# Spectral filter stage: planes loaded by halves, their negation on VectorE, a contiguous D eviction and a new order

## The chip, the core and the metric

The kernel runs on one core of a Trainium2 chip. The metric is the device time of one execution in microseconds. Three compute engines share the stage that the change touches: TensorE (PE), VectorE (DVE) and ScalarE (ACT). GpSimd (POOL) does small work and issues transfers on its own queue; SyncE (SP) issues the other transfers.

## The reference

Two blocks follow each other on a 2048 x 576 tensor. The change is in the first one, a global spectral filter.

```python
X = rfft2(layernorm(x).astype(float32), axes=(-2, -1))
W = w_r + 1j * w_i                       # 2048 x 289 each, bf16
h = x + irfft2(X * W, s=(S, D)).astype(bfloat16)
h2 = h + (gelu(n @ w_gate) * (n @ w_up)) @ w_down      # n = layernorm(h)
```

## The kernel before

Both transforms are matrix products. The spectrum is handled in 16 groups. For each group `i` the filter stage does the following: `D` (matmuls of the transform along d, evicted from PSUM to `CUS`), `B` (a 16-point transform, evicted to `YS`), `T` (the product with the filter, `TP`), `Z` (sums, `ZS` and `ZR`) and `V` (matmuls of the inverse 16-point transform, evicted to `V`). `R` does as `V` for the remaining columns of four groups at once, evicted to `VR`. `WS` holds three planes for each group: minus the imaginary part, the real part, the imaginary part. One product per group then gives the four terms of the complex multiplication.

```python
# SyncE's queue: the imaginary plane whole, then the real one; 18 loads each
for f in w_loads(1, 0, SP) + w_loads(1, 1, SP) + w_loads(0, 0, SP) + w_loads(0, 1, SP):
    f()
...
# D: the two banks (odd, even) one after the other, written with a step of two elements
ev(eng, CUS[:, s3, :, :].rearrange("p a (j r) -> p r a j", r=2), banks(b0, 2, 2 * HK)..., ...)
...
# GpSimd negates, group by group, then clears VR
for i in range(NG):
    P.op(POOL, ... tensor_scalar(WS[:, g, 0, :], WS[:, g, 2, :], -1.0, 1.0, op0=ALU.mult, op1=ALU.mult) ...)
    if i == NVZ:
        P.op(POOL, lambda g: g.memset(VR[:, :, :, :, :], 0.0), w=["Vz"])
for w in SEQF:            # the order of all operations of the stage
    ...
# next in GpSimd's queue: the first gate weights of the feed-forward block, 1.3 MB
for j in range(3):
    wg_load(j, j)
```

Operations are put into one queue for each engine in program order; each waits for the operations whose data it needs. So whatever stands later in an engine's program waits for what stands earlier, whether it needs it or not.

## Time and profile before

| | before |
|---|---|
| time, median | 496.69 us |
| first D matmul | 19.98 us |
| first product TP | 27.26 us |
| first matmul of the inverse transform (L684) | 52.44 us |
| first matmul of the feed-forward block (L824) | 64.77 us |
| from there to the end of the span | 430.13 us |

What precedes the first D matmul varies from one execution to another, 19.4 to 20.5 us. So I compare traces by one length: from the first D matmul to the first feed-forward matmul, 44.79 us here. I call it the stage length. It is a difference of two start times in the order of time of TensorE.

The busy time in two windows, up to L684 and from there to the feed-forward block, for the kernel before (columns: window, its length, then busy time and number of instructions of each engine, TensorE's granted clock, share of the DMA engines, GB/s):

```profile
20.00:52.40 32.40, 29.66 (x237) 21.71 (x234) 25.06 (x65) 29.19 (x52) 11.96 (x19) 1.00 0.58 171
52.40:64.80 12.40, 11.85 (x102) 8.68 (x104) 9.99 (x34) 10.25 (x24) 7.95 (x11) 1.00 1.02 363
```

In the first window VectorE is busy for 25.06 of 32.40 us, because it waits 6.70 us at the start. TensorE and ScalarE are busy for 29 us or more.

### The profile page before, as it was taken

To read this page: it belongs to the slowest core of one execution; us is meant where nothing else is said; L and a number is where in the kernel's file an instruction comes from. 1 tells how busy PE (TensorE), PEld (TensorE's weight loads), DVE (VectorE), ACT (ScalarE), POOL (GpSimd) and SP (SyncE) were. 2 spreads that over 40 slices of the span, in tenths; PEclk is the share of its full clock that TensorE was granted. 3 is DMA by queue.
4 is the path that set the end of the run, shared out by engine and by line. 5 is a ranking of instruction groups with operands and counts; after the bars stand their busy time and mean duration, and the time that the engine had idled before them with its cause. 6 is when DMAs were issued, how large, how long until landed. Compare 5 with 4: busy or idle time off the path is not lost.

```text
span 494.9 us, 9880 instructions
## 1 busy us (share of the span) xinstructions
PE 486.1 (98%) x4338; PEld 288.1 (58%) x4338; DVE 192.4 (39%) x418; ACT 158.9 (32%) x300; POOL 34.6 (7%) x53
## 2 busy tenths in 40 slices
PE   7999999999999999999999999999999999999998
PEld 3767655555588854444477744444677544444775
DVE  6679743444365644433311144333211233333111
ACT  6989865232312243232300033232100132233000
POOL 5750701000000010000000000000000000000000
DMA  8666898411000062000000001000000000000000
GB/s 276 163 188 215 277 350 275 178 25 27 4 13 13 19 191 60 19 9 1 1 13 19 18 15 23 19 1 1 7 19 12 14 1 1 1 1 2 12 19 19
DMA packets 27164, 31.26 MB, mean 63 GB/s; under 512 B 11664, under 2 KB 20112, under 8 KB 27120
## 3 DMA queue, kind: packets, MB, share of 16 engines
q1 hardware_dynamic: 24224, 18.68, 13.0%
q0 software_dynamic: 2896, 11.95, 7.1%
q8 instruction: 34, 0.56, 0.5%
q14 instruction: 10, 0.08, 0.1%
HBM read 26.28 MB, written 2.36 MB: 58 GB/s over the span
## 4 chain that ended last, share of the span: by engine, by line
PE 88%; DVE 4%; issue 1%; ACT 0%; DVEq 0%
PE PS L824 57%; PE PS L874 29%; DVE TP L594 1%; DVE VR L565 1%; PE PS L841 1%; PE PS L684 1%; PE PS L723 1%; DVE ZS L600 1%; DVE XO L726 0%; PE PS L855 0%; DVE ZR L603 0%; PE PS L610 0%; DVE HN L757 0%; PE PS L777 0%; DVE TM L734 0%
## 5 line engine op out<-in xcount | busy, mean ns | idle before, releaser
L824 PE MATMUL PS<-HT,WG 64*128 64x512 bf16 x2106 | 228.5, 376 | 0.0
L824 PEld LDWEIGHTS PS<-HT,WG 64*128 64x128 bf16 x2106 | 107.3, 94 | 119.8 <-issue 1.0
L833 ACT ACTIVATE GL<-PS 128x512 bf16<-128x512 f32 x144 | 85.9, 597 | 257.3 <-PE PS L824 243.4
L834 DVE TENSOR_TENSOR AT<-GL,PS 128x512 bf16<-128x512 bf16 x144 | 98.9, 687 | 175.0 <-ACT GL L833 175.0
L874 PE MATMUL PS<-WD,AT 128*128 128x288 bf16 (+2 forms) x1152 | 144.3, 286 | 0.0
L874 PEld LDWEIGHTS PS<-WD,AT 128*128 128x128 bf16 x1152 | 110.8, 98 | 30.7 <-ACT GL L833 1.3
L877 DVE TENSOR_TENSOR OS<-PS,XO 128x288 bf16<-128x288 f32 (+2 forms) x32 | 14.6, 457 | 100.3 <-PE PS L874 100.3
L824 PE MATMUL PS<-HT,WGX 64*128 64x512 bf16 x486 | 53.4, 376 | 0.0
L824 PEld LDWEIGHTS PS<-HT,WGX 64*128 64x128 bf16 x486 | 23.7, 94 | 28.8
L714 ACT ACTIVATE JD<-XO 128x576 bf16<-128x576 bf16 x8 | 5.5, 683 | 28.5 <-DVE XO L858 28.5
L594 DVE TENSOR_TENSOR TP<-YS,WS 128x1152 bf16<-128x1152 bf16 (+2 forms) x17 | 11.8, 715 | 6.8 <-DMA WS<-in_A_w_r_dram 6.7
L574 PE MATMUL PS<-FT,U 128*128 128x288 bf16 x96 | 14.1, 286 | 0.1
L565 ACT ACTIVATE CUS<-PS 128x576 bf16<-128x576 f32 x16 | 13.5, 862 | 0.5 <-PE PS L574 0.4
L565 ACT ACTIVATE YS<-PS 128x576 bf16<-128x576 f32 x16 | 11.3, 705 | 2.3 <-DVE TP L594 2.2
L520 PE MATMUL PS<-ATS,XO 128*128 128x128 bf16 (+1 forms) x128 | 10.1, 221 | 1.7 <-POOL XN L534 1.1
L584 PE MATMUL PS<-CUS,BT 128*128 128x288 bf16 x64 | 10.5, 286 | 1.2 <-ACT YS L565 0.9
L464 DVE BATCH_NORM_STATS2 ST<-XO 128x6 f32<-128x288 bf16 x24 | 9.3, 438 | 4.5 <-DMA XO<-in_A_x_dram 4.5
L574 PEld LDWEIGHTS PS<-FT,U 128*128 128x128 bf16 x96 | 9.1, 98 | 2.9 <-ACT CUS L565 0.4
L520 PEld LDWEIGHTS PS<-ATS,XO 128*128 128x128 bf16 (+1 forms) x128 | 7.4, 97 | 4.7 <-POOL XN L534 1.6
L610 PE MATMUL PS<-VT,ZS 128*128 128x256 bf16 x64 | 9.0, 273 | 1.1 <-DVE VR L565 0.5
L565 ACT ACTIVATE V<-PS 128x512 bf16<-128x512 f32 (+1 forms) x17 | 10.0, 639 | 0.3 <-PE PS L610 0.2
L757 DVE TENSOR_SCALAR HN<-XO,TM,RS 128x576 bf16<-128x576 bf16 (+1 forms) x32 | 10.0, 361 | 0.0
(77 smaller groups left out, 215.0 us busy)
## 6 DMA issues: line engine op xcount, KB each, us to landing
WD<-in_B_w_down_dram POOLq DMA_DIRECT2D x9, 576.0 KB, 21.4
WG<-in_B_w_gate_dram POOLq DMA_DIRECT2D x4, 1152.0 KB, 9.7
WG<-in_B_w_up_dram SPq DMA_DIRECT2D x4, 1152.0 KB, 7.9
out_dram<-OS SPq DMA_DIRECT2D x30, 72.0 KB, 1.6
XO<-in_A_x_dram SPq DMA_DIRECT2D x3, 576.0 KB, 7.4
WGX<-in_B_w_gate_dram POOLq DMA_DIRECT2D x1, 1152.0 KB, 6.9
WGX<-in_B_w_up_dram SPq DMA_DIRECT2D x1, 1152.0 KB, 10.8
HT<-HN SPq DMA_TRANSPOSE x60, 2.4
```

What stands on the lines that cost most here:

```text
L464: P.op(DVE, lambda v, c=c, h=h: v.bn_stats(ST1[:, c, h, :], XO[:, c, 288 * h:288 * h + 288]), r=[("X", c)], w=[("ST1", c, h)])
L520: P.op(PE, lambda t, b=b, lhs=lhs, p0=p0, p1=p1, s=s, e=e, o=o, c=c: t.matmul(bank(b, p0, p1, o, o + 128), lhs, ATS[:, c, :], start=s, sto ...
L565: fn = (lambda v: v.tensor_copy(dst, src)) if eng == DVE else (lambda a: a.activation(dst, src, ACTF.Copy))
L574: P.op(PE, lambda t, b=b, m=m, us=us, o=o, g=g: t.matmul(bank(b, 0, 128, 0, 2 * HK), U[:, us, g, :, :], FT[:, 3 * o + (2 if us == 4 else u ...
L584: P.op(PE, lambda t, b=b, tb=tb, m=m, s3=s3, sp_=sp_: t.matmul(bank(b, 0, 128, 0, KW), BT[:, sp_, tb, :], CUS[:, s3, m, :], start=(m == 0) ...
L594: P.op(DVE, lambda v: v.tensor_tensor(TP[:, sl, :, :, q0:q1], y4, w4, op=ALU.mult), r=[("Y", sl), ("Wn", i)] + wkeys[0 if 1 <= g < 9 else ...
L757: P.op(eng, lambda v, c=c, hs=hs, o0=o0, o1=o1, x0=x0, x1=x1: v.tensor_scalar(HN[:, hs, o0:o1], XO[:, c, x0:x1], TM[:, 1, c:c + 1], RS2[:, ...
L824: op = P.op(PE, lambda t, h0=h0, kt=kt, wt=wt, b=b, s=(not second and j == 0), e=(second and j == n - 1): t.matmul(bank(b), wg_tile(slot)[ ...
L833: P.op(ACT, lambda a: a.activation(GL[:, s2, :], bank(b0), ACTF.Gelu_apprx_tanh), r=[("PS", b0)], w=[("GL", s2)])
L834: P.op(DVE, lambda v: v.tensor_tensor(AT[:, f, :], GL[:, s2, :], bank(b0 + 1), op=ALU.mult), r=[("GL", s2), ("PS", b0 + 1)], w=[("AT", f)])
L874: P.op(PE, lambda t, b=b, d0=d0, d1=d1, f=f, p=p: t.matmul(bank(b, 0, 128, 0, d1 - d0), AT[:, f, 128 * p:128 * p + 128], WD[:, f, d0:d1], ...
L877: P.op(DVE, lambda v, b=b, d0=d0, d1=d1, p=p, c=c: v.tensor_tensor(OS[:, p % 2, d0:d1], bank(b, 0, 128, 0, d1 - d0), XO[:, c, d0:d1], op=A ...
```

## The change

Its intent: load the first half of both planes before the second half, so that the first product need not wait for ten loads that it does not use (the second half of the imaginary plane); take the negation off GpSimd and do it in a few large operations on VectorE; write the D eviction contiguously; spread evictions over both engines and find the orders again.

```diff
-    for f in w_loads(1, 0, SP) + w_loads(1, 1, SP) + w_loads(0, 0, SP) + w_loads(0, 1, SP):
+    for f in w_loads(1, 0, SP) + w_loads(0, 0, SP):
+        f()
+    P.dma(SP, VT..., "vt", w=["VT"])          # moved here from ahead of the planes
+    for f in w_loads(1, 1, SP) + w_loads(0, 1, SP):
         f()
...
-        ev(eng, CUS[...].rearrange("p a (j r) -> p r a j", r=2), banks(...).rearrange("p r (a j) -> p r a j", a=2),
+        ev(eng, CUS[...].rearrange("p a (j r) -> p a j r", r=2), banks(...).rearrange("p r (a j) -> p a j r", a=2),
...
+    def st_w(i):
+        for g0, g1 in (((1, 5),), ((5, 9),), ((9, 13),), ((13, 16), (0, 1)))[i]:
+            P.op(DVE, ... tensor_scalar(WS[:, g0:g1, 0, :], WS[:, g0:g1, 2, :], -1.0, None, op0=ALU.mult),
+                 r=[k for k in wkeys[i // 2] if k[2] == 1], w=[("Wn", 4 * i + k) for k in range(4)])
...
-    for i in range(NG):
-        P.op(POOL, ... 16 negations ...)
-        if i == NVZ:
-            P.op(POOL, lambda g: g.memset(VR[:, :, :, :, :], 0.0), w=["Vz"])
+    P.op(POOL, lambda g: g.memset(VR[:, :, :, :, :], 0.0), r=[("ATS", c) for c in range(NT)], w=["Vz"])
...
-SEQF = """D0 D1 B0 D2 D3 T0 B1 D4 ... Z15b Z15a R3 V15 R4"""
+SEQF = """w0 D0 D1 D2 B0 B1 w1 T0 T1 D3 D4 Z0 B2 B3 Z1 D5 T2 T3 B4 w2 Z2 T4 ... V14 V15 R4 R3"""
+# and a table of the engine of each eviction: VectorE takes one D, two B, three V and seven VR
```

(The last V eviction is now one operation.)

## The prediction

> **What bounds the kernel now.** First the page, its chain that ended last, to see who sets the end.
>
> ```profile
> PE 88%; DVE 4%; issue 1%; ACT 0%; DVEq 0%
> PE PS L824 57%; PE PS L874 29%; DVE TP L594 1%; DVE VR L565 1%; PE PS L841 1%; PE PS L684 1%; PE PS L723 1%; DVE ZS L600 1%; DVE XO L726 0%; PE PS L855 0%; DVE ZR L603 0%; PE PS L610 0%; DVE HN L757 0%; PE PS L777 0%; DVE TM L734 0%
> ```
>
> 85% of the span is the feed-forward part (L824, L874), TensorE back to back, which the change does not touch. The same chain in order of time shows where it can act:
>
> ```profile
> 51.91 0.39 ACT V L565
> 52.30 0.14 issue
> 52.44 1.63 PE PS L684 x12
> ...
> 64.77 70.11 PE PS L824 x648
> ```
>
> The filter ends at 52.44 us, when the inverse transform (L684) may start; 12.3 us later TensorE starts the feed-forward part and no longer waits. So the change is worth what it moves that 52.44, microsecond for microsecond, if the 12.3 us after it stay. Before 51.9 the chain is almost all VectorE: TP (spectrum times filter), ZS and ZR (sums), VR (a cast). Next VectorE in order of time:
>
> ```profile
> 18.16 2.40 DVE L529 CAST U<-PS 128x384 bf16<-128x384 f32 x5
> 27.26 1.43 DVE L594 TENSOR_TENSOR TP<-YS,WS 128x1152 bf16<-128x1152 bf16 x2 [6.70 <-DMA WS<-in_A_w_r_dram]
> ```
>
> VectorE finishes the first transform at 20.56 and stands idle 6.70 us until the first half of the real filter plane lands. Then it works almost without a gap until 52.95. Meanwhile ScalarE goes from 21.07 to 52.57 with 2.9 us idle. The groups by shape in the first 130 us give the pieces:
>
> ```profile
> L565 ACT ACTIVATE CUS<-PS 128x576 bf16<-128x576 f32 x16 | 13.5, 862 | 0.5 <-PE PS L574 0.4
> L565 ACT ACTIVATE YS<-PS 128x576 bf16<-128x576 f32 x16 | 11.3, 705 | 2.3 <-DVE TP L594 2.2
> L594 DVE TENSOR_TENSOR TP<-YS,WS 128x1152 bf16<-128x1152 bf16 x15 | 10.9, 751 | 6.8 <-DMA WS<-in_A_w_r_dram 6.7
> L565 DVE CAST VR<-PS 32x256 bf16<-32x256 f32 x15 | 6.3, 418 | 0.3
> L632 POOL TENSOR_SCALAR WS<-WS 128x288 bf16<-128x288 bf16 x16 | 6.9, 431 | 2.2 <-DVE ATS L494 0.9 <-POOL WS L632 0.2
> ```
>
> These durations overlap by some 0.1 us; for a queue I take start to start from the order of time: CUS 0.67, YS 0.52, V 0.47, TP 0.68, ZS plus ZR 0.44, VR 0.43 us, and on TensorE 0.73 (D), 0.49 (B), 0.45 (V) and 0.22 (R).
>
> **What the Trainium skill says.** "VectorE: DVE Perf Modes", The perf-mode tier table: a one-source bf16 operation within SBUF may run four elements a cycle, and one reading PSUM may not. The trace agrees: in the same window, HN at L757 averages 424 ns for 576 columns and 303 for 64, so 0.24 ns a column. "SBUF — State Buffer", Who interferes with whom: such an operation shares a port pair with GpSimd, and the second to issue blocks until the first ends; the trace of before has no such pair on which I could test it. "PSUM — Partial Sum Buffer", Specifications: cachelines are 8 bytes and non-contiguous patterns slow matmuls. It says nothing of evictions that hop between two banks; no run here shows it yet. "DMA: Bandwidth & Descriptors", Queues, rings and completion order: engines take turns between queue rows by packet, yet a completion increment waits for earlier writes of the engine across its queues. The trace shows the delay, whichever of the two makes it:
>
> ```profile
> WS<-in_A_w_i_dram SPq DMA_DIRECT2D x2, 36.0 KB, 2.2
> WS<-in_A_w_r_dram SPq DMA_DIRECT2D x2, 36.0 KB, 6.5
> ```
>
> Same size, but the second pair was issued at 30.9 us, just after GpSimd's 1.3 MB gate load (30.10).
>
> **The change part by part.**
>
> *Load order.* The SyncE queue issues a filter load every 0.70 us (18 in 12.57 us). Before, 18 imaginary loads stand ahead of the real ones: eight real ones issue from 19.5, the last lands at 27.2. Now the eight of the first half follow at once: imaginary from 6.2 to 11.8, real to 17.4, landed by about 20.5 (landing took 3 to 4 us there). The 6.70 us wait goes. It is not worth 6.70: the first product needs YS. TensorE starts D at 19.98. D0 ends by 21; its eviction, 0.7; B0 after D2, 0.65; eviction 0.65. So TP starts near 23.6, a head start of 3.7 us.
>
> *Negation.* 16 operations of 431 ns leave GpSimd, where they were off the chain. Five instructions (the fourth step is two) arrive on VectorE. By the column rate above, 1152 columns take about 0.45 us start to start (estimate): 1.9 us. The first is likely to meet the VR memset, which now runs on GpSimd about 18.4 to 21.9 (3.52 us in before), so TP may start at 24.1 instead.
>
> *Contiguous D eviction.* CUS has the shape of YS but costs 0.67 instead of 0.52. If writing contiguous and reading the two banks alternately costs as YS does, each saves 0.14 us; ScalarE saves 16 x 0.14 = 2.2 us.
>
> *New distribution.* VectorE's casts from PSUM: by U at 128x384 (five in 2.40, so 0.47) and 1.04 ns a column, 0.60 for V and 0.67 for D or B. ScalarE after: 15 D x 0.53 + 14 B x 0.52 + 13 V x 0.47 + 9 VR x 0.38 = 24.8 us, against 16 x (0.67 + 0.52 + 0.47) + 0.4 = 27.0. VectorE after: 16 x 1.12 + 7 VR x 0.43 + 3 V x 0.60 + 3 x 0.67 + 1.9 = 26.6, against 17.9 + 15 x 0.43 = 24.4. TensorE: 16 x 1.67 + 5 x 0.22 = 27.8 from 19.98, so never before 47.8. Unlike before, the three are nearly level.
>
> *Sum.* VectorE has 1.6 us of its 26.6 behind it when the first TP starts (24.1), so 25.0 follow; before, it lost 1.3 us in small gaps (27.26 to 52.95 is 25.7 for 24.4). I allow 1.0: VectorE ends at 50.1, and L684 starts near 50.0. That is 2.4 us earlier.
>
> *A piece given back.* GpSimd no longer negates until 26.6, so its gate load, behind the memset in its queue, issues near 22 instead of 30.10, amid the second half's loads (imaginary issued 17.9 to 24.8). By the 6.5 us above the last lands near 29 to 30 instead of 27. The third negation waits for all ten. By my count VectorE reaches it at 28: three or four products and two sums after 24.1. That stall, 1 to 1.5 us if it comes, lies on the fullest engine. I charge 0.4 after weighing it at about a third: some of it would fall into gaps that the queue has anyway. Gain 2.0 us; with the timed 496.69, 494.7; I round to 494.6.
>
> **The rivals.** (1) *The stall at the third negation comes whole.* For it: the 6.5 us. Against: the order was searched and may know the landing. VectorE has 21 us left after it; from 30 that ends at 51 to 52: gain 0.5 to 1, time near 496. (2) *The alternate-bank read is slow.* For it: no page or trace clears it. If D costs 0.3 us more instead of 0.14 less, ScalarE has 31 us from 21.8, ends at 53, and all is lost: 496.5 to 497.5. I give it one in ten. (3) *TensorE becomes the bound and the rest hides under it.* It needs 27.8 us, and its pipeline fill and tail cost at least 1.5, so the end is near 49.3 and the time 493.5. This is the best that a good order can reach. (4) *The load was hidden anyway.* Speaking for it: ScalarE and TensorE were at work during VectorE's wait. Against: ScalarE too stopped at 26.2 for 1.8 us, until TP released YS.
>
> **Range and chances.** Rival 3 gives the low edge, 493.2; rivals 1 and 2 the high one, 496.4. A change of 2% would be 9.9 us, more than the whole wait and all savings that I found; slower by 2% would need the filter to be a third longer. So 0.98 for same.
>
> **What would show it.** First TP at 23.6 to 24.3 and no wait for the real plane; mean CUS near 705 ns; L684's first start near 50.4 instead of 52.44, and L824's 12.3 us behind it. Third negation: its wait, and for which load. First negation: whether it begins only when the VR memset ends. Where ScalarE has the gaps and VectorE none, VectorE is the bound; gaps on both mean that TensorE or the order is. I am wrong if CUS exceeds 862 ns, if a wait for WS over 1.5 us shows on VectorE, or if the part from L684 to L824 lengthens.

## The result

The changed kernel took 497.57 us (median of 4; 497.20 to 498.12), the kernel before 496.70. The ratio is 1.0019, with a 95% interval of 1.0001 to 1.0036. (A ratio here is the mean time of one kernel's runs over that of the other's in the same rounds, so not quite the ratio of the medians that I quote.) The change makes the kernel slower by a little less than 0.9 us; I had forecast a gain of 2.1 us.

The order of time of VectorE in the changed kernel, around the start of the products:

```profile
20.64 1.65 DVE L603 TENSOR_SCALAR WS<-WS 128x1152 bf16<-128x1152 bf16 x1
22.21 0.74 DVE L569 CAST CUS<-PS 128x576 bf16<-128x576 f32 x1
22.88 0.44 DVE L603 TENSOR_SCALAR WS<-WS 128x1152 bf16<-128x1152 bf16 x1
24.54 1.43 DVE L598 TENSOR_TENSOR TP<-YS,WS 128x1152 bf16<-128x1152 bf16 x2 [1.22 <-ACT YS L569]
...
26.98 1.43 DVE L598 TENSOR_TENSOR TP<-YS,WS 128x1152 bf16<-128x1152 bf16 x2
31.12 0.46 DVE L603 TENSOR_SCALAR WS<-WS 128x1152 bf16<-128x1152 bf16 x1 [2.71 <-DMA WS<-in_A_w_i_dram]
```

The first product starts at 24.54 instead of 27.26; the wait of 6.70 us is gone, as intended. But a new one stands four products later: the third negation waits 2.71 us for the imaginary plane. The waits of the stage, longest first in total (waiting engine and line, what it waited for, total, times, longest):

```profile
POOL WG L220 <- DVE TP L598: 28.0, 1, 28.0
ACT YS L569 <- DVE TP L598: 2.8, 1, 2.8
DVE WS L603 <- DMA WS<-in_A_w_i_dram: 2.7, 1, 2.7
PEld PS L588 <- DVE YS L569: 2.4, 1, 2.4
PE PS L588 <- DVE YS L569: 2.1, 1, 2.1
```

The first line costs nothing: GpSimd has a later load to issue and nothing else to do. The others are one event. VectorE stands still for 2.7 us, ScalarE waits for the product that frees `YS`, and TensorE waits 2.1 us for an eviction that VectorE does late.

Why does the load come late? Two lines of the view by transfer, for the loads issued from 17.9 to 23.7 us (transfer, issuer, number, size, median time to landing), show it:

```profile
WS<-in_A_w_i_dram SPq DMA_DIRECT2D x8, 63.0 KB, 2.4
WS<-in_A_w_i_dram SPq DMA_DIRECT2D x2, 36.0 KB, 7.0
```

Ten loads of the second half follow each other in SyncE's queue. The first eight land in the usual 2.4 us, and the last two, though smaller, in 7.0. In between, GpSimd issued the gate weights:

```profile
18.47 3.52 POOL L642 MEMSET VR<- 128x4096 bf16 x1 [0.84 <-DVE ATS L492]
21.92 1.51 POOL L220 DMA_DIRECT2D WG<-in_B_w_gate_dram  x2
```

Before, 16 negations and the clearing of `VR` stood ahead of this load, and it was issued at 30.10. With the negations gone it is issued at 21.92. This is the theory that the experiments test. The inverse transform follows at 53.05 instead of 52.44 and the feed-forward block at 66.04 instead of 64.77: the stage length is 45.91 us, 1.12 more than before.

### The profile page after: what moved, and what is told of

Read it like the earlier page. It is cut to its first block, busy times and chain, and to the rows that moved or that the text cites. A ratio compares the mean times of both kernels' runs of the same rounds, so it can differ in the third digit from the quotient of the medians.

```text
span 496.1 us, 9860 instructions
## 1 busy us (share of the span) xinstructions
PE 485.7 (98%) x4337; PEld 289.0 (58%) x4338; DVE 195.8 (39%) x421; ACT 157.1 (32%) x301; POOL 27.6 (6%) x37
## 4 chain that ended last, share of the span: by engine, by line
PE 88%; SPq 4%; DVE 4%; DMA 1%; issue 1%; ACT 0%; DVEq 0%
PE PS L833 56%; PE PS L883 29%; SPq L220 4%; DMA WS<-in_A_w_i_dram 1%; DVE TP L598 1%; PE PS L850 1%; DVE ZS L609 1%; PE PS L693 1%; PE PS L732 1%; DVE XO L735 0%; PE PS L864 0%; DVE VR L569 0%; DVE ZR L612 0%; DVE YS L569 0%; DVE WS L603 0%
## 5 line engine op out<-in xcount | busy, mean ns | idle before, releaser
L883 PEld LDWEIGHTS PS<-WD,AT 128*128 128x128 bf16 x1152 | 110.8, 98 | 30.7 <-ACT GL L842 1.3
L833 PEld LDWEIGHTS PS<-HT,WGX 64*128 64x128 bf16 x486 | 23.7, 94 | 28.7
L518 PE MATMUL PS<-ATS,XO 128*128 128x128 bf16 (+1 forms) x128 | 10.1, 221 | 1.8 <-POOL XN L532 1.3
L569 ACT ACTIVATE CUS<-PS 128x576 bf16<-128x576 f32 x15 | 9.7, 650 | 1.6 <-PE PS L578 1.1
L569 ACT ACTIVATE YS<-PS 128x576 bf16<-128x576 f32 x14 | 8.9, 653 | 3.3 <-DVE TP L598 2.8
L867 DVE SCALAR_TENSOR_TENSOR XO<-PS,XO 128x576 bf16<-128x576 f32 x8 | 6.1, 758 | 8.0 <-PE PS L864 8.0
```

Of the source, the lines that this page charges most:

```text
L518: P.op(PE, lambda t, b=b, lhs=lhs, p0=p0, p1=p1, s=s, e=e, o=o, c=c: t.matmul(bank(b, p0, p1, o, o + 128), lhs, ATS[:, c, :], start=s, sto ...
L569: fn = (lambda v: v.tensor_copy(dst, src)) if eng == DVE else (lambda a: a.activation(dst, src, ACTF.Copy))
L833: op = P.op(PE, lambda t, h0=h0, kt=kt, wt=wt, b=b, s=(not second and j == 0), e=(second and j == n - 1): t.matmul(bank(b), wg_tile(slot)[ ...
L883: P.op(PE, lambda t, b=b, d0=d0, d1=d1, f=f, p=p: t.matmul(bank(b, 0, 128, 0, d1 - d0), AT[:, f, 128 * p:128 * p + 128], WD[:, f, d0:d1], ...
```

## The experiments

Twelve kernels ran in three groups, each group on one chip with its own runs of the kernel before. The theory: the gate load, which nobody meant to move, holds up the second half of the imaginary plane, and VectorE, which takes the third negation in order, stands still for it. Rivals: A, the load is late by its own place in the queue; B, the wait costs nothing and the new order does; and, beside both, VectorE, now fuller, is the bound.

### Hold the gate load back

```diff
+    P.op(POOL, None, r=[k for k in wkeys[1] if k[2] == 1])     # wait for the second half of the imaginary plane
     for j in range(3):
         wg_load(j, j)
```

> The changed kernel, in which GpSimd waits for the ten second-half loads of the imaginary plane before it issues its 1.3 MB gate load. Theory (the gate load, issued at 21.92 us instead of 30.10, holds those ten loads up and the third negation waits 2.71 us for them): their last lands near 26.5 us instead of 31.1, the third negation waits under 0.3 us, L693 starts 2 to 2.7 us earlier, near 50.5, and the time falls from 497.6 to about 495.0. Rival A (the loads come late by their place in the queue): landing and wait stay, 497.5. Rival B (the wait is not what costs, the new order and the fuller VectorE are): the wait goes but the time stays above 496.7.

Measured: 495.24 us (before 496.63; ratio 0.9973, interval 0.9958 to 0.9988). The gate load is issued at 27.21 us and VectorE meets the third negation without a wait. The lines of its order of time:

```profile
26.55 1.43 DVE L598 TENSOR_TENSOR TP<-YS,WS 128x1152 bf16<-128x1152 bf16 x2
27.89 0.53 DVE L603 TENSOR_SCALAR WS<-WS 128x1152 bf16<-128x1152 bf16 x1
```

The stage length is 43.35 us, 2.56 less than in the changed kernel. One added wait on an idle engine turns the loss of 0.9 us into a gain of 1.4. The loads land in time in the same place of the same queue, so rival A falls; the time is below 496.7, so rival B falls too.

The packets that moved from 24 to 28 us show that the transfers themselves were held up. First the changed kernel, then the one with the gate held (queue, packets, MB, share of the 16 engines' time):

```profile
q0 software_dynamic: 288, 1.24, 84.5%
q1 hardware_dynamic: 205, 0.10, 10.1%
```

```profile
q1 hardware_dynamic: 652, 0.32, 37.7%
```

q0 is GpSimd's queue and q1 SyncE's. Beside the gate load SyncE's queue moved 205 packets in these 4 us, without it 652. A packet of the gate load carries 1.24 MB / 288 = 4.3 KB and one of the planes 0.10 MB / 205 = 0.5 KB. From 25.5 to 28 us GpSimd's queue moves 201 packets and SyncE's 204: the turns are equal and the time is not, since the small packets have 16.1% of it and the large ones 86.9%. From 24 to 25.5 us there are no equal turns: the gate load moves 87 packets and SyncE's queue one. No run shows why. Nor do these counts tell whether late completions, the other way that the prediction names, add to the delay.

### Take the negation later instead

```diff
-SEQF = "... B4 w2 Z2 T4 ... D9 V3 w3 Z6 ... B9 T8 ... T11 B12 ..."
+SEQF = "... B4 Z2 T4 ... D9 V3 Z6 ... B9 w2 T8 ... T11 w3 B12 ..."
```

> The changed kernel with the gate load as it is, but the third negation moved behind the eighth product (just ahead of the ninth, the first that needs it) and the fourth just ahead of the thirteenth. Theory (a wait taken too early in VectorE's order): the landing stays near 31, VectorE does not wait at that place, and the time falls to about 495.2, nearly as with the gate held. If VectorE was going to idle anyhow for want of YS (rival: the wait only filled a gap), the time stays at 497.

Measured: 496.15 us (495.61 to 497.10; before 496.63, ratio 0.9992, interval 0.9975 to 1.0009). The two last loads still land in 6.5 us, and VectorE no longer waits for them, as expected. The stage length is 43.98 us, 1.93 less than in the changed kernel and 0.63 more than with the gate held. So the wait was not a filler. I expected 495.2 and the median missed that by 0.9; the profiled execution was also one that reached the first D matmul late, at 20.53, and the slowest one, 497.10, shows a mean clock of 0.997 (the others 1.000). Where the remaining 0.63 us go I did not settle: VectorE shows only small waits for ScalarE and TensorE.

### Move the gate load in the kernel before

The same cause put into the other kernel: two transfers moved, nothing else.

```diff
     for i in range(NG):
         P.op(POOL, ... negation ...)
+        if i == 7:
+            P.dma(POOL, WG3[:, 0, 0:4, :], ...)          # the gate half of wg_load(0, 0), not issued later
+            P.dma(POOL, WG3[0:64, 0, 8, :], ...)
```

> The kernel before, with the first gate load issued by GpSimd after its eighth negation (near 22.4 us) instead of at 30.1; nothing else changed. Theory: the real plane's loads that are in flight then land with the gate load, near 29.5 to 30.5 instead of 27.2, VectorE's wait for the first product grows from 6.7 to 9.5 us, and the time rises from 496.7 to about 499.5. Rival (the two queues share the engines packet by packet and small loads hardly suffer): the first product stays within 0.7 us of 27.3, time 496.7 to 497.3.

Measured: 501.69 us (ratio 1.0102, interval 1.0084 to 1.0121), and VectorE's first wait, of 6.7 us in the kernel before, becomes

```profile
DVE TP L594 <- DMA WS<-in_A_w_r_dram: 10.6, 1, 10.6
```

The first product starts at 31.01. The cause costs more here than in the changed kernel since here the held-up loads stood on the path already. It cost more than I expected (499.5). The wait was 10.6 us where I had 9.5. And TensorE paused for 4.83 us and its granted clock then fell to half. Four windows of one microsecond after the pause (columns as above, the clock third from the end):

```profile
32.00:33.00 1.00, 0.49 (x3) 0.32 (x4) 1.00 (x4) 1.00 (x2) 0.00 (x0) 0.50 0.77 152
33.00:34.00 1.00, 1.00 (x6) 0.64 (x5) 0.98 (x3) 1.00 (x3) 0.00 (x0) 0.50 0.97 358
34.00:35.00 1.00, 1.00 (x6) 0.65 (x5) 0.98 (x3) 0.86 (x2) 0.00 (x0) 0.50 0.99 384
35.00:36.00 1.00, 1.00 (x9) 0.71 (x8) 0.97 (x3) 0.87 (x2) 0.00 (x0) 0.83 0.98 382
```

All four executions of this kernel have a mean clock of 0.993 to 0.997, so its time is the cause and this together. In the profiled one, the fastest, the clock adds little: the first product comes 3.91 us later after the first D matmul than before, and the stage length is 4.14 us longer (48.93). The two at 0.993 took 502.15 and 502.65 us and were not profiled.

### The load order alone

```diff
-NVZ = 15
+NVZ = 7              # VR is cleared after the eighth negation, no longer after the last
     ...              # and the loads as in the change: both first halves, VT, both second halves
```

> The kernel before with the half-by-half load order alone; GpSimd still negates, and clears VR after its eighth negation, so its gate load issues only near 31 us. Theory: the first product starts near 23.5 to 24 us instead of 27.26; VectorE carries 24.4 us and no negation, so the filter ends 2 to 3 us earlier and the time is 493.8 to 494.8: the load order alone beats both kernels. Rival C (GpSimd's last eight negations, now beside VectorE's two-input products, block each other on the shared port): TP longer than 0.80 us or negations longer than 0.6 us while they overlap, time above 495.5. Rival D (the load was hidden anyway): time within 0.5 of 496.7.

Measured: 495.31 us (before 496.63; ratio 0.9974, interval 0.9960 to 0.9989), stage length 43.86. One part of the change, with `VR` cleared earlier, beats both kernels, but by less than I expected (493.8 to 494.8). Here the negations on GpSimd keep the gate load back by chance: it is issued at 32.57. The expectation's rival C also showed, in the durations:

```profile
27.05 5.56 POOL L634 TENSOR_SCALAR WS<-WS 128x288 bf16<-128x288 bf16 x8 [1.67 <-DMA WS<-in_A_w_i_dram]
```

The last eight negations run beside VectorE's products and take 5.56 us for eight instead of 4.02, up to 914 ns for one, and `ZR` takes 0.41 us instead of 0.18 where they meet. So there was a reason to take the second half of the negation off GpSimd. What this collision costs in time was not measured.

### Clear VR later

The first negation took 1.65 us, the second 0.44, for the same shape. The first starts at 20.64 while GpSimd clears `VR` until 21.99.

```diff
     (with the gate held for the imaginary plane, as above)
-    P.op(POOL, lambda g: g.memset(VR[:, :, :, :, :], 0.0), r=[("ATS", c) for c in range(NT)], w=["Vz"])
     ... st_w(i)
+            if i == 1:
+                P.op(POOL, lambda g: g.memset(VR[:, :, :, :, :], 0.0), r=[("Wn", 7)], w=["Vz"])
```

> The changed kernel with the gate load held, and GpSimd's clearing of VR moved behind VectorE's second negation. Theory (the first negation took 1.65 us instead of 0.44 because it had to wait for the clearing of VR to end): the first negation takes about 0.45 us and the first product starts about 1 us sooner after the first D matmul (3.3 to 3.9 us instead of 4.42); the time falls below the 495.24 of the run with the gate held by 0.4 to 1.0. Rival (the long first negation comes from the load or the plane's layout): it stays at 1.65. If it shortens but the time stays within 0.3, the head start is lost further down, in TensorE or in the order.

Measured: the first negation takes 0.44 us, and the first product starts 3.87 us after the first D matmul instead of 4.42.

```profile
20.16 0.44 DVE L603 TENSOR_SCALAR WS<-WS 128x1152 bf16<-128x1152 bf16 x1
```

"SBUF — State Buffer", Who interferes with whom, which the prediction could not test, agrees for this pair: the negation that met GpSimd's clearing of `VR` took 1.65 us instead of 0.44, and the two ended 0.3 us apart. Not every operation of VectorE is blocked: here the first two products run beside the clearing (21.93 to 25.45 us) in their usual 1.43 us.

The median is 494.89 us (before 496.69; ratio 0.9972), 0.35 under the 495.24 of the gate held where I expected 0.4 to 1.0. But the four executions were 496.09, 494.95, 494.69 and 494.84, and the profile fell on the slow one. It shows why:

```profile
DVE TP L598 <- DMA WS<-in_A_w_r_dram: 2.2, 1, 2.2
```

The gate load, held only for the imaginary half, now ran into the real half, and the ninth product waited for that. It is the same event one plane later.

### Undo the contiguous eviction, and do it alone

```diff
-        ... "p a (j r) -> p a j r" ...        (first run: in the changed kernel with the gate held)
+        ... "p a (j r) -> p r a j" ...        (second run, the reverse: in the kernel before)
```

> The changed kernel with the gate load held, but the D eviction written in the old, strided order. ScalarE's D operation goes from 654 back to some 820 ns, 0.14 us more from start to start for 15 of them, 2.1 us of ScalarE. If ScalarE is the bound of the changed filter, the time rises by 1 to 2 us over 495.24; if VectorE is (the reading of the prediction, 26.6 us against 24.8), it rises by under 0.6.

> The kernel before with the contiguous D eviction alone. D falls from 862 (or 820) to about 655 ns, ScalarE is relieved of 2.2 us; VectorE still starts at 27.3 and has the longest queue, so the time stays at 496.6 within 0.4. If ScalarE was a bound in the kernel before too, it falls by 0.7 or more.

Measured: undone, 495.38 us against 495.24 with the gate held (ratios to before 0.9983 and 0.9973, from two groups), stage length 43.83 against 43.35. Alone in the kernel before, 496.50 us against 496.69 (ratio 0.9999, interval 0.9984 to 1.0014). ScalarE's D eviction does what was hoped for; the same line in the kernel before and in the second run:

```profile
L565 ACT ACTIVATE CUS<-PS 128x576 bf16<-128x576 f32 x16 | 13.5, 862 | 0.5 <-PE PS L574 0.4
```

```profile
L565 ACT ACTIVATE CUS<-PS 128x576 bf16<-128x576 f32 x16 | 10.5, 665 | 0.7 <-PE PS L574 0.4
```

ScalarE is busy 3.0 us less and the time does not move: VectorE has the longer queue there. This part is worth at most the 0.5 us of stage length in the changed order, and no time that these runs can tell from none. Even the 0.5 need not be its own: the profile of the first run also shows a wait of 0.6 us for the real plane, as in the section before.

### A version that beats both

The first eight negations go back to GpSimd, where nothing collides with them; the gate load is held.

> A version meant to beat both: the changed kernel with the gate load held, the first eight negations back on GpSimd (where nothing of VectorE's collides with them before 22 us) ahead of the clearing of VR, the last two steps of negation left on VectorE. VectorE loses 0.9 us of work and the block of 1.2; its eviction of the first D starts at 20.6 instead of 22.2 and the first product 3.3 to 3.8 us after the first D matmul. Time 494.0 to 494.9. If it stays at 495.2, TensorE or ScalarE bound the filter and VectorE's relief is worth nothing.

Measured: 495.25 us (494.91 to 496.00; before 496.69, ratio 0.9976), above the 494.0 to 494.9 that I expected. The stage length of the profiled execution is 42.95, the shortest so far, but the executions lie 1.1 us apart, and the profile shows a wait of 0.39 us for the real half. So the last group held the gate load for both planes, in three versions, and ran the changed kernel beside them.

```diff
-    P.op(POOL, None, r=[k for k in wkeys[1] if k[2] == 1])
+    P.op(POOL, None, r=wkeys[1])                               # the second half of both planes
```

> The changed kernel with one line more: GpSimd holds its gate load until the second half of both planes has landed (near 33.5 us). With the gate held for the imaginary half alone the gate load still ran beside the real half's loads (landings of 5 to 6 us), and VectorE met no wait for them in that profile. Theory: the time is 494.9 to 495.3, as with the half hold, but the runs lie closer together. If the remaining gate traffic cost something on the path, it falls by 0.5 or more.

> Gate held for both planes, and VR cleared behind VectorE's second negation. In the run with the half hold the profile showed a wait of 2.2 us for the real half in front of the ninth product, and that execution was the slowest of four (496.09 against 494.69 to 494.95). Theory: that wait goes, no execution is above 495.5, and the median is 494.2 to 494.9, 0.3 to 0.8 below the gate held alone. If the median equals the gate held alone, the block of the first negation was off the path.

> Gate held for both planes, the first eight negations on GpSimd, the rest on VectorE. Same theory as with VR cleared later, and VectorE has 0.9 us less to do: 493.9 to 494.8. If it equals the version with all negations on VectorE, VectorE's 0.9 us are worth nothing, TensorE and the order bound the stage.

> The changed kernel once more, on the same chip as the three repairs, for a comparison of the same rounds: 497.2 to 498.1, that is 0.5 to 1.4 slower than before; the repair by the gate alone should lie 2 to 2.8 us below it.

| kernel, five executions each | median (range), us | ratio to before | stage length, us |
|---|---|---|---|
| before (nine) | 496.81 (496.52 to 497.08) | | 44.79 |
| changed, again | 497.58 (497.13 to 498.92) | 1.0021 | 47.24 |
| gate held for both planes | 495.01 (494.53 to 495.19) | 0.9963 | 43.36 |
| the same, VR cleared later | 494.40 (494.19 to 494.82) | 0.9953 | 42.78 |
| the same, half of the negation on GpSimd | 494.56 (494.27 to 494.91) | 0.9956 | 42.74 |

(The stage length of before is that of its own profile.) Holding the gate for both planes takes the scatter away from the versions with `VR` cleared later and with half of the negation on GpSimd: their executions lie 0.63 and 0.64 us apart instead of 1.40 and 1.09. The gate held alone had none to lose (0.59 before, 0.66 now). Clearing `VR` later is worth 0.58 us of stage length and 0.61 of the median. Half of the negation on GpSimd spares VectorE 0.9 us and gains nothing. That does not show that VectorE's load is no bound, though: the 0.9 us lie ahead of the first product, where VectorE then waits instead (0.51 us for the first D and 1.99 for `YS`, against 1.64 for `YS` alone), and the first product starts 3.85 us after the first D matmul instead of 3.87. The best version runs in 494.40 us, 0.5% under the kernel before (interval of the ratio 0.9941 to 0.9966), with the change's parts all kept and two operations of GpSimd put elsewhere.

The changed kernel's profiled execution, 498.92 us, is its slowest and shows the clock once more. TensorE pauses there for 2.06 us behind VectorE's wait, and then:

```profile
34.00:35.00 1.00, 1.00 (x6) 0.63 (x5) 0.97 (x3) 0.97 (x3) 0.00 (x0) 0.50 1.03 392
35.00:36.00 1.00, 1.00 (x6) 0.59 (x5) 1.00 (x4) 0.42 (x1) 0.00 (x0) 0.50 0.94 321
36.00:37.00 1.00, 1.00 (x7) 0.68 (x5) 1.00 (x2) 0.74 (x2) 0.00 (x0) 0.50 1.02 348
37.00:38.00 1.00, 1.00 (x9) 0.74 (x8) 0.94 (x5) 0.51 (x1) 0.00 (x0) 0.79 1.06 398
```

The first profile of the changed kernel had the same pause (2.07 us) and a clock of 1.00 throughout. Up to the end of the pause the two run alike: it ends 13.90 and 13.91 us after the first D matmul. So the clock adds 47.24 - 45.91 = 1.3 us to some executions; the other four here show a mean clock of 1.000.

## Why the prediction was wrong

**The bound and the lever** were right. The change is worth what it moves the end of the filter. The 430 us from the feed-forward block on did not move; the 12.3 us between did, as told below.

**Load order.** The 6.70 us went. The first product was to start at 23.6, or at 24.1 if the first negation met the clearing of `VR`; it met it and started at 24.54, counted from a first D matmul 0.15 us later than before.

**Contiguous D.** The size was right (650 ns, as `YS`), and so was that it is not on the path. The rival of a slow alternate-bank read fell (CUS above 862 ns was to be the sign).

**The piece given back** is the step that failed, and it failed in its size. The prediction said that the gate load "issues near 22 instead of 30.10", that the last load "lands near 29 to 30", that VectorE reaches it at 28, and then: "I charge 0.4 after weighing it at about a third". The load was issued at 21.92, the last landed at 31.1, VectorE arrived at 28.4 and stood for 2.71 us. Removing this by the gate alone is worth 497.57 - 495.24 = 2.3 us, and 2.56 of stage length. So nearly the whole wait was on the path, and the term was 0.4 where it measured 2.3 (2.57 in the last group, with both planes held: 497.58 - 495.01). The mechanism had been read from the trace of before, with a number (6.5 us beside the gate load). It needed no luck to happen: the program order of GpSimd fixes it. Two things made it small. First the landing was summed wrongly: ten loads at 0.70 us from 17.9 start the last one at 24.2, and 24.2 + 6.5 is 30.7, not 29 to 30. With VectorE there at 28, the stall by the prediction's own numbers is 2.7 us, not 1 to 1.5. Then a third of it was charged. A weight of a third belongs to a thing that may or may not happen; this one was sure, and only its size was open. I also argued that some of it would fall into gaps that the queue has anyway; the run with the gate held shows hardly any gap there.

**The rest of the sum** was too high by a smaller amount. Without the stall I expected a gain of 2.4 us; the gate held gives 1.4. The trace of that run splits the difference. From the first D matmul to the inverse transform are 30.39 us where 30.0 was predicted. And the part behind, 12.33 us before, is 12.96 there (12.99 in the changed kernel), where I assumed that it stays. It goes with the new order and its table of engines: it is 12.33 to 12.38 us in the four kernels with the old ones (before, the gate early, the load order alone, the contiguous D alone) and 12.96 to 12.99 in all with the new ones. Where it comes from is read in the chain that ended last of the changed kernel:

```profile
52.36 0.76 PE PS L631 x4
53.14 0.37 ACT VR L569
53.52 0.38 ACT VR L569
53.91 0.05 issue
53.95 1.28 PE PS L693 x9
```

In the new order both `R` steps come last, and ScalarE evicts two parts of `VR` one after the other behind them. The inverse transform starts with three matmuls at 53.05 and then waits for `VR` until 53.95. No run put the `R` steps elsewhere, so that they are the reason is not shown. Nor is the cause of the other 0.39 us. (Two small things in the sum change nothing: 494.7 was rounded to 494.6, and the 1.04 ns a column of VectorE's casts stands without a source. The trace of the kernel before gives 1.06, from `U` with 384 and with 256 columns, 541 and 405 ns.) Two of the signs of being wrong that the prediction had named came true: a wait for `WS` over 1.5 us on VectorE, and this longer part.

**The rivals.** The first, the stall that comes whole, was the one that happened, and I had put its time "near 496": it comes out 1.5 us worse. It had VectorE go on at 30 and 12.3 us follow the filter; VectorE went on at 31.12, and 12.99 us followed. These two, 1.1 and 0.7 us, cover the difference. Whether TensorE became the bound (the third rival) is open. With the gate held, from the first D matmul to the inverse transform (columns as above):

```profile
19.70:50.10 30.40, 28.83 (x238) 22.26 (x236) 28.29 (x68) 26.69 (x51) 4.99 (x6) 1.00 0.62 182
```

TensorE is busy 28.83 us of 30.40 and VectorE 28.29, so the two are level, and no run relieves one of them behind the first product. The best version has 29.79 us for this part; that rival's sum was 27.8 + 1.5 = 29.3.

## What to carry to other kernels

Taking work off an idle engine is not free if that engine's queue also issues transfers: whatever stood behind the work now goes earlier, and may run into loads that are waited for. When a change shortens a queue, list what moves up, and give each transfer an explicit wait instead of a place in line. And when a mechanism and its time are read from the trace, do the sum with that time, and charge it whole.

## What the Trainium skill lacked or had wrong

- "DMA: Bandwidth & Descriptors", Queues, rings and completion order, says that an engine takes turns between queues by packet. The trace's packet counts agree from 25.5 to 28 us (201 and 204), not from 24 to 25.5 (87 and 1). The page lacks the consequence: loads with packets of 0.5 KB beside one with 4.3 KB got 10.1% of the engines' time in 4 us, moved 205 packets instead of 652, and the last two landed in 7.0 us instead of 2.8.
- "PSUM — Partial Sum Buffer" warns of non-contiguous patterns for matmuls and says nothing of evictions that read or write in such a pattern. ScalarE read two banks alternately, element by element, in 650 ns where a plain read of the same shape (`YS`) took 653; writing bf16 with a step of two elements to SBUF instead took 826 to 862. No page gives a time for either on ScalarE.
- "TensorE: Matmul & The Clock Gate", What's actually happening, lets the clock fall after at least one idle window of about 3.4 us, and calls the window free-running. The clock records in the packed traces agree on the window: in the second profile of the changed kernel they read 1.0 for 27.307 us, 0.5 for 3.413 and 1.0 again, and 27.307 is 8 x 3.413. But the window that halved the clock was not idle throughout. It ran from 30.59 to 34.00 us by this count, and TensorE paused in it for 2.06 us, from 31.64 to 33.70. In the first profile, whose records start at 6.33, a window ends at 33.64 and cuts the pause of 2.07 us into 1.67 and 0.40, and the clock stayed at 1.0. So 2.06 us of pause in one window were enough and 1.67 were not, in one profile each.
